# Tail and attention loop of a backward kernel: PSUM banks, eviction engine, store queues, and the order of loads and stores

## The chip, the cores and the metric

The kernel runs on one core of one Trainium2 chip. The metric is the device time of one execution in microseconds, lower is better. TensorE (PE), VectorE (DVE), ScalarE (ACT) and GpSimd (POOL) compute; SyncE (SP) only issues DMAs. SP, ScalarE and GpSimd each have a queue of DMAs of their own, and an engine's queue is worked off in order: an instruction that waits holds up everything behind it.

## The reference

The reference returns the output and nine gradients of a transformer block with modulated layer norms (batch 1, 2048 tokens, 512 features, 32 heads of 16, inner width 1792, bf16):

```
mod = silu(c) @ w_mod                      # sa, ca, ga, sb, cb, gb
h = layernorm(x) * (1 + ca) + sa
x = x + ga * attention(h, wqkv, wo)
h = layernorm(x) * (1 + cb) + sb
x = x + gb * (relu(h @ w1 + b1)**2 @ w2 + b2)
out, vjp = jax.vjp(block); return out, *vjp(grad_out)
```

The change touches the backward pass of the attention and what comes after it: with E = exp(scores), dS = (dO V^T) * E, the loop makes dV = E^T dO, dK = dS^T Q and dQ = dS K for each head. The tail makes dh1 = [dQ dK dV] Wqkv^T, the gradient of the first layer norm (output 1), dWqkv = h1^T [dQ dK dV] (output 2), and the gradients of c (output 8) and w_mod (output 9).

## The kernel before

The forward pass and the backward pass of the dense part come first and are not touched. Then two stages follow, and in both the instructions of every engine stand in the order in which the program writes them.

**The loop.** The 32 heads go in eight groups (`hg`, called heads here) of four. A head has 64 units: four blocks of 512 keys (`kc`), times 16 blocks of 128 queries in four groups (`qc`, `qi`). A unit is four score products (`psS_A`, `psS_B`, `psS_C`, line 1578), four exponentials on ScalarE (`expo`, `E_u`, line 1584), two calls of `dp_pair` (each two products `psD_u` and one product with `E_u` on VectorE, line 1600), the products into `accVK`, and a transpose of `dS_u` (`transpose_unit`), mostly by a DMA on SP's queue: 32 blocks of 128 x 128 every second unit, or 16 blocks. Two blocks of units later the transposed `dsT` is multiplied with K into `dqacc` (`dq_quad`, line 1667), which ScalarE scales and GpSimd adds up (`dq_out`, line 1685); after a head's last block the sum lies in `dQst`.

A written list of letters gives the order of these steps within a block. A counter `j` counts the calls of `dp_pair`, 128 to a head; `at(j, ...)` puts a step behind call `j`. What is put there are DMAs on ScalarE's queue (`load`, line 1560): the 22 loads of the next head (`plan_head`), the stores of `vkb` to `dVKtP`, the four stores of `dQst` to `dQc`, and towards the end pieces of what the tail reads (`pieces`) and rows of the transposed weight (`w_rows`). The DMAs of the SP and ScalarE queues share eight semaphores in turn.

**The tail.** `dh1(t)` adds 11 or 12 products of 512 columns for token tile `t` of 16 into a PSUM bank: first those whose sources are on the chip (`early7`), then `late`, of which `dq` 3 comes last. Tiles with `t % 6 < 2` have a bank of their own (`psx`); the others are halves of a two-bank tile of `psd`. For each tile ScalarE makes `xn1b` (`norm_tile`), VectorE two products with sums and a small scaling (`ln_grad`), ScalarE `tqa`, VectorE `uqa` (`dx_out`), which GpSimd's queue adds to output 1. `mod_row` spreads rows of earlier sums over the partitions (`pmod`), `wmod_grad` makes output 9 (`dwms`). `turn_vk` turns four sources on TensorE (`tokA`), `turn_dma` four more by DMA (`tokB`) and later the four of `dq` into `KS_tok`, over the weight rows that `dh1` has read. Then twelve groups of 16 products (`dwqkv`, line 1967) make dWqkv in the order `tokA`, `tokB`, `KS_tok`; between them stand the last row sums, `c_grad` with the loaded `w_mod`, and `c_out`. Each group is copied into `wqblk` (three buffers) and stored.

The names of the DMAs' sources and targets in the profile are those of the reused tiles: `ik`, `iv`, `iq`, `ido` and `qz` hold `dq` and `vk` sources in the tail.

Of the kernel before, what the change touches and what calls it, by code (L numbers as in the profile page):

```python
# [20 lines left out]
P = 128  # L21
# [13 lines left out]
def kernel(  # L35
# [1491 lines left out]
    dqw = hold.enter_context(tc.tile_pool(name="phIw", bufs=2))  # L1527
    psd = hold.enter_context(tc.tile_pool(name="psId", bufs=2, space=bass.MemoryType.PSUM))
    psx = hold.enter_context(tc.tile_pool(name="psIx", bufs=1, space=bass.MemoryType.PSUM))
# [6 lines left out]
    with ExitStack() as ph:  # L1536
        ework = ph.enter_context(tc.tile_pool(name="phIe", bufs=4))
        units = [(hg, kc, qc, qi) for hg in range(HG) for kc in range(QC) for qc in range(QC) for qi in range(4)]
        NU = len(units)
# [22 lines left out]
        def plan_head(hg):  # L1562
            j0 = (hg - 1) * 128 + 14
            loads = list(kvq_loads(hg)) + list(row_loads(hsets[hg % 2]["do"], dOT_st, hg, slice(0, n), d_st))
            for i, (to, fro) in enumerate(loads):
                at(j0 + 4 * i, load, to, fro)
            at(j0 + 40, spread_qz, hg)
# [102 lines left out]
        def dq_out(b):  # L1670
# [15 lines left out]
            if kc == QC - 1 and qc == QC - 1 and hg < HG - 1:  # L1686
                for hq in range(4):
                    r = hg % 2 * 64 + hq * DH
                    at(cur["j"] + 6 + hq, load, dQc[hg // 2, r:r + DH, :], st["dq"][32 * hq:32 * hq + DH, :])

# [23 lines left out]
        with tc.manual_schedule(engines={PE.engine, ACT.engine, DVE.engine, SP.engine, POOL.engine}):  # L1714
# [49 lines left out]
            late = (("dq", 1), ("vk", 4), ("dq", 2), ("vk", 5), ("dq", 3))  # L1764
            pds, pair = {}, {}

            def acc_of(t):
                if t not in pds:
                    if t % 6 < 2:
                        pds[t] = psx.tile([P, 512], F32, name="pdh1", tag=f"ps{t % 6}")[:]  # L1770
                    else:
                        if t % 2 == 0:
                            pair["t"] = psd.tile([P, 2, 512], F32, name="pdh2", tag="pd")
                        pds[t] = pair["t"][:, t % 2, :]
                return pds[t]
# [9 lines left out]
            def turn_vk(i):  # L1785
                pt = psd.tile([P, TT, P], BF, name="ptv", tag="pd")
                for t in range(TT):
                    PE.transpose(pt[:, t, :], xs["vk", i][:, t * P:(t + 1) * P], identb[:])
                for g in range(2):
                    DVE.tensor_copy(tokA[:, i, 8 * g:8 * g + 8, :], pt[:, 8 * g:8 * g + 8, :])  # L1790

# [39 lines left out]

    with ExitStack() as ph:
        big = ph.enter_context(tc.tile_pool(name="phJbig", bufs=1))
        rec1, rec4 = (hsets[i]["qs"].rearrange("p t e -> p (t e)").bitcast(F32) for i in range(2))
# [17 lines left out]
        def constants():  # L1852
            POOL.memset(thirty2[:], 1.0 / 32)
            POOL.tensor_copy(selb[:], identb.rearrange("p (j c) -> p j c", c=32)[:, :, 0:1].to_broadcast([P, 4, P]))
            POOL.tensor_copy(rowsb[0:97, :], sums[0:97, :])
            DVE.scalar_tensor_tensor(out=nb1[:], in0=mean1[:], scalar=-1.0, in1=rstd1[:], op0=ALU.mult, op1=ALU.mult)

# [12 lines left out]
        def wmod_grad(ic, js, k):  # L1870
            buf = dwms[:, ic % 2]
            ACT.activation(buf[:, k, :], dmodb[:, js[k], :], AF.Identity, scale=siluc_f[:, ic:ic + 1])
            if k == len(js) - 1:
                SP.dma_start(out=out_9[ic * P:(ic + 1) * P, js[0] * D:(js[-1] + 1) * D].rearrange("p (j d) -> p j d", d=D),
                             in_=buf[:, 0:len(js), :])
# [82 lines left out]
        def dwqkv(n, b, ic):  # L1958
            if n % 4 < 2:
                if n % 4 == 0:  # L1960
                    accs["p"] = psd.tile([P, 2, 512], F32, name="pwq", tag="pd")
                pw = accs["p"][:, n % 2, :]
            else:
                pw = psx.tile([P, 512], F32, name="pwx", tag=f"ps{n % 2}")[:]
            for t in range(TT):
                rhs = KS_tok[:, t, 0:D] if b == 0 else (tokA if b == 1 else tokB["t"])[:, :, t, :]
                PE.matmul(pw, h1J[:, t, ic * P:(ic + 1) * P], rhs, start=(t == 0), stop=(t == TT - 1))
            wblk = big.tile([P, D], BF, name="wqblk", tag="xn1b", bufs=3)
            rows = out_2[ic * P:(ic + 1) * P, :]
            if b == 0:  # L1970
                ACT.activation(wblk[:, 0:256], pw[:, 0:256], AF.Identity)
                DVE.tensor_copy(wblk[:, 256:512], pw[:, 256:512])
                SP.dma_start(out=rows[:, 0:D], in_=wblk[:])
            else:
                for i in range(2):
                    srcv = pw.rearrange("p (g v d) -> p g v d", v=2, d=DH)[:, :, 1 - i, :]
                    dstv = wblk[:, i * 256:(i + 1) * 256].rearrange("p (g d) -> p g d", d=DH)
                    if i == 0:
                        ACT.activation(dstv, srcv, AF.Identity)
                    else:  # L1980
                        DVE.tensor_copy(dstv, srcv)
                dst = rows[:, D:3 * D].rearrange("p (v c) -> p v c", v=2)[:, :, (b - 1) * 256:b * 256]
                SP.dma_start(out=dst, in_=wblk.rearrange("p (v c) -> p v c", v=2))

# [10 lines left out]
        with tc.manual_schedule(engines={PE.engine, ACT.engine, DVE.engine, SP.engine, POOL.engine}):  # L1995
            for g in range(3):
                load_x0(g)
            constants()
            turn_vk(1)
            last_dq(B_last, slice(3 * 512, n))  # L2000
            turn_vk(2)
            turn_vk(3)
# [5 lines left out]
            for t in range(2, 6):  # L2008
                dh1(t, early7)
                if t < 4:  # L2010
                    mod_row(3 * (t - 2))
            load_x0(3)
            for t in range(TT):
# [3 lines left out]
                ln_grad(t)  # L2017
                if t in (1, 3):
                    mod_row((t + 1) // 2)
                if t > 0:  # L2020
# [3 lines left out]
                if t >= 8:  # L2024
                    wmod_grad(t // 4 - 2, (2, 3, 4, 5), t % 4)
                if t < 8 and t % 2 == 0:
                    turn_dma("vk", 4 + t // 2)
                if t in (6, 8, 10, 11):
                    g = (6, 8, 10, 11).index(t)
                    dma(h1J[:, 4 * g:4 * g + 4, :], h1_st[:, 4 * g:4 * g + 4, :])  # L2030
                if t % 4 == 3 and t > 4:
                    row_sums(t // 4 - 1)
            for i in range(4):
                load_wmod(i)
                turn_dma("dq", i)
            order = [(b, ic) for b in (1, 2, 0) for ic in range(DC)]
            cg = [(j, ic) for j in (2, 3, 4, 5, 0, 1) for ic in range(DC)]
            for k, (b, ic) in enumerate(order):
# [16 lines left out]
                elif k < 8:  # L2055
                    wmod_grad(k - 4, (0, 1), 0)
                    wmod_grad(k - 4, (0, 1), 1)
                if k == 10:
                    c_out()

# [61 lines left out]
```

## Time and profile before

| what | value |
|---|---|
| median of 3 runs | 2514.32 us (2510.01, 2514.43 and the median) |
| profiled execution, its own time | 2511.93 us |
| its span, first to last instruction | 2510.1 us |
| TensorE busy | 2311.6 us (92%) |
| ScalarE busy | 2297.3 us (92%) |
| VectorE busy | 1812.8 us (72%) |
| GpSimd busy | 361.0 us (14%) |
| mean granted TensorE clock | 0.984 |
| loop | about 1118 to 2374 us of the span |
| tail | about 2374 to 2510 us of the span |

Busy times are of the one profiled execution; durations in what follows are from it too. A name with q behind it (ACTq, SPq) is the sequencer of that engine, which issues DMAs. A bracket behind a row gives the idle time of the engine before it and what ended it.

### The profile page before, as it was taken

The page shows a single profiled execution, that of the slowest core. Times are in us where ns is not written, and L with a number is a line of the kernel's source. Part 1 is how long each engine was busy: PE and PEld are TensorE (multiplying, and loading weights), DVE is VectorE, ACT ScalarE, POOL GpSimd, SP SyncE. Part 2 cuts the span into 40 slices and gives each one's busy share as a digit, 9 for nine tenths or more (in the row PEclk, how much of TensorE's full clock was granted, in tenths as well). Part 3 has the DMA queues.
Part 4 walks back from the last instruction along what each step waited for, and adds up shares of the span by engine and source line. Part 5 has one row for each costly group of instructions (what it writes and reads, how often), then busy time and mean ns, then how long its engine had stood idle before and what let it go on. Part 6 is the DMA issues. An engine that isn't in the chain of part 4 may idle for free.

```text
span 2510.1 us, 49480 instructions
## 1 busy us (share of the span) xinstructions
PE 2311.6 (92%) x18745; PEld 767.3 (31%) x18826; DVE 1812.8 (72%) x2366; ACT 2297.3 (92%) x3574; POOL 361.0 (14%) x393
## 2 busy tenths in 40 slices
PE   8898799989988998999999999999999999999987
PEld 3232223223322323432223322233232333223333
DVE  6555153454435454579999989999999999989864
ACT  7999999999989999539999999999999999999852
POOL 2000001211322242110111101111010110100110
PEclk9999999999999999999999999999999999999998
DMA  4467454367658765969999999999999999999975
GB/s 146 128 168 176 150 124 128 90 169 144 94 91 176 146 145 113 270 198 195 205 201 200 201 205 208 192 208 202 205 201 209 210 206 206 207 197 204 208 175 152
DMA packets 1224858, 442.37 MB, mean 176 GB/s; under 512 B 1099246, under 2 KB 1197548, under 8 KB 1224364
## 3 DMA queue, kind: packets, MB, share of 16 engines
q1 hardware_dynamic: 1189788, 398.06, 81.8%
q0 software_dynamic: 13120, 18.88, 5.4%
q10 hardware_dynamic: 21712, 22.27, 3.5%
q8 instruction: 148, 2.42, 0.4%
q14 instruction: 90, 0.74, 0.1%
HBM read 94.63 MB, written 70.78 MB: 66 GB/s over the span
## 4 chain that ended last, share of the span: by engine, by line
ACT 40%; PE 38%; issue 8%; DVE 6%; DMA 4%; SPq 1%; ACTq 1%; POOL 0%; another core or an unknown queue 0%; DVEq 0%; POOLq 0%
ACT E_u L1584 24%; ACT ET L566 12%; PE dqacc L1667 4%; PE psST L564 4%; PE psS_A L1578 3%; PE pm L232 3%; PE accVK L1640 2%; DMA dsT<-dS_u 2%; ACT dsT L1754 2%; PE psS_B L1578 2%; PE oacc L580 2%; PE psS_C L1578 2%; PE pm L413 2%; PE pm L399 2%; PE accVK L1649 2%
## 5 line engine op out<-in xcount | busy, mean ns | idle before, releaser
L1600 DVE TENSOR_TENSOR dS_u<-psD_u,E_u 128x1024 bf16<-128x1024 f32 x1024 | 1186.1, 1217 | 71.0 <-PE psD_u L1598 17.2
L566 ACT ACTIVATE ET<-psST 128x1024 bf16<-128x1024 f32 x1024 | 941.3, 1254 | 20.4 <-PE psST L564 20.2
L1584 ACT ACTIVATE E_u<-psS_A 128x512 bf16<-128x512 f32 x768 | 510.8, 665 | 11.1 <-DMA d_st<-dltT 7.3
L1584 ACT ACTIVATE E_u<-psS_B 128x512 bf16<-128x512 f32 x768 | 504.1, 656 | 13.0 <-DMA dsT<-dS_u 6.7
L1598 PE MATMUL psD_u<-iv,ido 32*128 32x512 bf16 x2048 | 408.4, 386 | 0.0
L564 PE MATMUL psST<-qt_sb,kt_sb 32*128 32x512 bf16 x2048 | 319.6, 385 | 61.2 <-ACT ET L566 46.9
L1584 ACT ACTIVATE E_u<-psS_C 128x512 bf16<-128x512 f32 x512 | 334.1, 652 | 6.6 <-DMA dsT<-dS_u 2.9
L1578 PE MATMUL psS_B<-ik,iq 32*128 32x512 bf16 x768 | 293.5, 382 | 15.9 <-ACT E_u L1584 8.6
L1578 PE MATMUL psS_A<-ik,iq 32*128 32x512 bf16 x768 | 292.1, 380 | 11.7 <-ACT E_u L1584 1.1
L1578 PEld LDWEIGHTS <-iq 32*128 32x128 bf16 x2048 | 130.3, 91 | 316.4 <-issue 298.7
L1640 PE MATMUL accVK<-dS_u,qz 128*32 128x512 bf16 x2048 | 212.5, 390 | 0.3 <-PE psD_u L1598 0.3
L580 PE MATMUL oacc<-ET,vaug 128*32 128x512 bf16 x2048 | 207.4, 395 | 3.2 <-DVE ostage L584 3.2
L1685 POOL TENSOR_TENSOR dQacc<-dQacc,dqtmp 128x512 f32<-128x512 f32 x64 | 81.3, 1270 | 852.0 <-ACT dqtmp L1680 790.3
L1649 PE MATMUL accVK<-E_u,dOs_tok 128*16 128x512 bf16 x2048 | 203.2, 386 | 0.0
L1578 PE MATMUL psS_C<-ik,iq 32*128 32x512 bf16 x512 | 194.6, 380 | 4.1 <-ACT dqtmp L1680 0.2
L564 PEld LDWEIGHTS <-kt_sb 32*128 32x128 bf16 x2048 | 86.4, 91 | 349.9 <-issue 325.4
L1667 PE MATMUL dqacc<-dsT,KS_tok 128*32 128x512 bf16 x2048 | 145.8, 382 | 17.9 <-ACT E_u L1584 3.8
L1754 ACT ACTIVATE dsT<-ptT 128x1024 bf16<-128x1024 bf16 x126 | 144.2, 1145 | 1.8 <-PE ptT L1630 1.6
L250 DVE COPY part<-pm 128x512 f32<-128x512 f32 (+2 forms) x103 | 63.5, 616 | 113.6 <-PE pm L232 103.5
L1598 PEld LDWEIGHTS <-ido 32*128 32x128 bf16 x2048 | 104.8, 91 | 99.4 <-issue 93.3
L1640 PEld LDWEIGHTS <-qz 128*32 128x32 bf16 x2048 | 57.9, 94 | 177.7 <-issue 162.8
L584 DVE COPY ostage<-oacc 128x512 f32<-128x512 f32 x32 | 22.1, 689 | 101.4 <-PE oacc L580 85.2
(417 smaller groups left out, 2512.3 us busy)
## 6 DMA issues: line engine op xcount, KB each, us to landing
p_st<-part POOLq DMA_DIRECT2D x36, 256.0 KB, 5.3
kt_sb<-qkT_st SPq DMA_DIRECT2D x124, 64.0 KB
wA<-in_B_w_dram SPq DMA_DIRECT2D x28, 256.0 KB
wB<-w1T_st SPq DMA_DIRECT2D x21, 256.0 KB
wA<-w2T_st SPq DMA_DIRECT2D x21, 256.0 KB
wB<-in_B_w_dram SPq DMA_DIRECT2D x21, 256.0 KB
p_st<-part POOLq DMA_DIRECT2D x25, 192.0 KB, 4.6
p_st<-part SPq DMA_DIRECT2D x18, 256.0 KB
```

Of the source, the lines that this page charges most:

```text
L564: PE.matmul(ps[:, hi, :], kt_sb[r:r + 32, kt * P:(kt + 1) * P], qt_sb[r:r + 32, :], start=True, stop=True, tile_position=(r, 0))
L566: ACT.activation(ET[:, 2 * pair:2 * pair + 2, :], ps[:], AF.Exp, scale=SCALE)
L580: PE.matmul(oacc[32 * hq:32 * hq + 32, :], lhsT, ET[:, hq, :], start=(kt == 0), stop=(kt == TT - 1), tile_position=(0, 32 * hq), skip_grou ...
L1578: PE.matmul(psS[:], st["q"][r:r + 32, qt * P:(qt + 1) * P], st["k"][r:r + 32, kc * 512:kc * 512 + 512], start=True, stop=True, tile_positi ...
L1584: ACT.activation(bst[u][0][:, hq, :], sst.pop((u, hq))[:], AF.Exp, scale=SCALE)
L1598: PE.matmul(psD[:, hi, :], st["do"][r:r + 32, qt * P:(qt + 1) * P], st["v"][r:r + 32, kc * 512:kc * 512 + 512], start=True, stop=True, til ...
L1600: DVE.tensor_tensor(dS_u[:, 2 * pair:2 * pair + 2, :], psD[:], E_u[:, 2 * pair:2 * pair + 2, :], ALU.mult)
L1640: PE.matmul(cur["vk"][32 * hq:32 * hq + 32, :], hst[hg]["qz"][:, qt, hq, :], bst[u][1][:, hq, :], start=(qt == 0), stop=False, tile_positi ...
L1649: PE.matmul(acc[32 * hq:32 * hq + DH, :], dOs_tok[:, qt, (hg * 4 + hq) * DH:(hg * 4 + hq + 1) * DH], E_u[:, hq, :], start=False, stop=(qt ...
L1667: PE.matmul(acc[32 * hq:32 * hq + 32, :], KS_tok[:, kc * 4 + kt, h * DH:h * DH + 32], tT[:, :, hq * 4 + kt, :], start=(kt == 0), stop=(kt ...
L1685: POOL.tensor_tensor(dst2, dst, tmp[:], ALU.add)
L1754: ACT.activation(dst, pt[:], AF.Identity)
```

## The change

In the loop, the first four loads of the next head stay at calls 14, 18, 22 and 26 of the head; the other 18 move from calls 30 to 98, four apart, to calls 50 to 111, about 3.6 apart. The four stores of dQ move from four consecutive calls (the sixth to ninth after the last sum) to calls 30, 34, 38 and 42 of the head after.

In the tail, the two-bank pool `psd` ends with the loop and four single banks (`psJn`) take its place: every token tile of `dh1`, every half of `turn_vk` and every group of `dwqkv` has a bank to itself. ScalarE alone copies dWqkv out of PSUM; `wqblk` has three buffers of its own instead of sharing them with `xn1b`. The stores of `wqblk` (but the last) and of `dwms` go to GpSimd's queue. The constants stand behind the last dQ sum on GpSimd, with the one VectorE step split off (`nb1_rows`). The `mod_row` steps move from among the early `dh1` products behind token tiles 1 to 4. The loads of `h1` come at tiles 0, 2, 3 and 4 instead of 6, 8, 10 and 11, the transposes of `tokB` at 6, 8, 10 and 12 instead of 0, 2, 4 and 6. All `w_mod` loads go ahead of the four transposes into `KS_tok`, with which they alternated. `c_grad` goes by blocks of `ic`, and `c_out` stands behind the last group instead of ahead of it. The twelve copies of `dwqkv` on VectorE are gone.

```diff
-    psd = hold.enter_context(tc.tile_pool(name="psId", bufs=2, space=bass.MemoryType.PSUM))
+        psd = ph.enter_context(tc.tile_pool(name="psId", bufs=2, space=bass.MemoryType.PSUM))
...
-                at(j0 + 4 * i, load, to, fro)
+                at(j0 + (4 * i if i < 4 else 36 + 36 * (i - 4) // 10), load, to, fro)
...
-                    at(cur["j"] + 6 + hq, load, dQc[hg // 2, r:r + DH, :], st["dq"][32 * hq:32 * hq + DH, :])
+                    at(hg * 128 + 158 + 4 * hq, load, dQc[hg // 2, r:r + DH, :], st["dq"][32 * hq:32 * hq + DH, :])
...
-                        if t % 2 == 0:
-                            pair["t"] = psd.tile([P, 2, 512], F32, name="pdh2", tag="pd")
-                        pds[t] = pair["t"][:, t % 2, :]
+                        pds[t] = banks4["p"].tile([P, 512], F32, name="pdh2", tag="pn", bufs=4)[:]
...
+        banks4["p"] = ph.enter_context(tc.tile_pool(name="psJn", bufs=4, space=bass.MemoryType.PSUM))
...
-                SP.dma_start(out=out_9[ic * P:(ic + 1) * P, js[0] * D:(js[-1] + 1) * D].rearrange("p (j d) -> p j d", d=D),
+                POOL.dma_start(out=out_9[ic * P:(ic + 1) * P, js[0] * D:(js[-1] + 1) * D].rearrange("p (j d) -> p j d", d=D),
...
-            if n % 4 < 2:
-                if n % 4 == 0:
-                    accs["p"] = psd.tile([P, 2, 512], F32, name="pwq", tag="pd")
-                pw = accs["p"][:, n % 2, :]
+            if n % 3 < 2:
+                pw = banks4["p"].tile([P, 512], F32, name="pwq", tag="pn", bufs=4)[:]
             else:
-                pw = psx.tile([P, 512], F32, name="pwx", tag=f"ps{n % 2}")[:]
+                pw = psx.tile([P, 512], F32, name="pwx", tag=f"ps{n // 3 % 2}")[:]
...
-            wblk = big.tile([P, D], BF, name="wqblk", tag="xn1b", bufs=3)
+            wblk = big.tile([P, D], BF, name="wqblk", tag="wqblk", bufs=3)
+            queue = SP if n == 11 else POOL
             if b == 0:
-                ACT.activation(wblk[:, 0:256], pw[:, 0:256], AF.Identity)
-                DVE.tensor_copy(wblk[:, 256:512], pw[:, 256:512])
-                SP.dma_start(out=rows[:, 0:D], in_=wblk[:])
+                ACT.activation(wblk[:], pw, AF.Identity)
+                queue.dma_start(out=rows[:, 0:D], in_=wblk[:])
...
-            constants()
+            nb1_rows()
             turn_vk(1)
             last_dq(B_last, slice(3 * 512, n))
+            constants()
...
-                if t < 4:
-                    mod_row(3 * (t - 2))
...
-                if t in (1, 3):
-                    mod_row((t + 1) // 2)
+                if 1 <= t < 5:
+                    mod_row(t - 1)
...
-                if t < 8 and t % 2 == 0:
-                    turn_dma("vk", 4 + t // 2)
-                if t in (6, 8, 10, 11):
-                    g = (6, 8, 10, 11).index(t)
+                if t in (6, 8, 10, 12):
+                    turn_dma("vk", 1 + t // 2)
+                if t in (0, 2, 3, 4):
+                    g = (0, 2, 3, 4).index(t)
...
             for i in range(4):
                 load_wmod(i)
+            for i in range(4):
                 turn_dma("dq", i)
...
-            cg = [(j, ic) for j in (2, 3, 4, 5, 0, 1) for ic in range(DC)]
+            cg = [(j, ic) for js in ((2, 3, 4, 5), (0, 1)) for ic in range(DC) for j in js]
...
-                if k == 10:
-                    c_out()
+            c_out()
```

More of the change, by code (lines that the diff above doesn't have):

```diff
@@ L1764 @@
             late = (("dq", 1), ("vk", 4), ("dq", 2), ("vk", 5), ("dq", 3))
-            pds, pair = {}, {}
+            pds, banks4 = {}, {}
             def acc_of(t):
@@ L1785, in turn_vk @@
             def turn_vk(i):
-                pt = psd.tile([P, TT, P], BF, name="ptv", tag="pd")
-                for t in range(TT):
-                    PE.transpose(pt[:, t, :], xs["vk", i][:, t * P:(t + 1) * P], identb[:])
                 for g in range(2):
-                    DVE.tensor_copy(tokA[:, i, 8 * g:8 * g + 8, :], pt[:, 8 * g:8 * g + 8, :])
+                    if "p" in banks4:
+                        pt = banks4["p"].tile([P, 8, P], BF, name="ptv", tag="pn", bufs=4)
+                    else:
+                        pt = psd.tile([P, 8, P], BF, name="ptw", tag="pd")
+                    for i8 in range(8):
+                        t = 8 * g + i8
+                        PE.transpose(pt[:, i8, :], xs["vk", i][:, t * P:(t + 1) * P], identb[:])
+                    DVE.tensor_copy(tokA[:, i, 8 * g:8 * g + 8, :], pt[:])
             def copy_turn(half):
@@ L1855, in constants, with nb1_rows @@
             POOL.tensor_copy(rowsb[0:97, :], sums[0:97, :])
+        def nb1_rows():
             DVE.scalar_tensor_tensor(out=nb1[:], in0=mean1[:], scalar=-1.0, in1=rstd1[:], op0=ALU.mult, op1=ALU.mult)
@@ L1976, in dwqkv @@
                     srcv = pw.rearrange("p (g v d) -> p g v d", v=2, d=DH)[:, :, 1 - i, :]
[L1977 to L1981, printed above, removed]
+                    ACT.activation(wblk[:, i * 256:(i + 1) * 256].rearrange("p (g d) -> p g d", d=DH), srcv, AF.Identity)
                 dst = rows[:, D:3 * D].rearrange("p (v c) -> p v c", v=2)[:, :, (b - 1) * 256:b * 256]
-                SP.dma_start(out=dst, in_=wblk.rearrange("p (v c) -> p v c", v=2))
+                queue.dma_start(out=dst, in_=wblk.rearrange("p (v c) -> p v c", v=2))
         def turn_dma(key, i):
```

## The prediction

> **What bounds the kernel now.** I read the page first, then busy time by stretches, then for each stretch that is not full the waits, the timeline of the engine that holds it and the chain of waits.
>
> ```profile
> ACT 40%; PE 38%; issue 8%; DVE 6%; DMA 4%; SPq 1%; ACTq 1%; POOL 0%; another core or an unknown queue 0%; DVEq 0%; POOLq 0%
> ```
>
> The chain alternates between ScalarE and TensorE, so no one engine is the bound all along. The columns of the next view are the stretch, its length, and the busy us (and instructions) of PE, weight loads, DVE, ACT and POOL, then TensorE's granted clock, DMA share, GB/s. The first two rows are two heads of the attention loop (128 steps of two products `psD_u`, called pairs here, 1.21 us each), the others the tail.
>
> ```profile
> 1273.00:1428.00 155.00, 149.34 (x1450) 47.05 (x1451) 148.55 (x129) 153.50 (x294) 17.98 (x13) 1.00 1.21 201
> 1428.00:1583.00 155.00, 146.55 (x1396) 45.47 (x1389) 143.26 (x125) 148.28 (x283) 17.98 (x13) 0.98 1.18 203
> ...
> 2374.00:2401.30 27.30, 21.54 (x193) 11.34 (x192) 12.73 (x17) 7.08 (x10) 3.79 (x5) 0.94 0.94 217
> 2401.30:2443.20 41.90, 35.88 (x171) 14.69 (x169) 33.58 (x90) 27.24 (x37) 8.49 (x7) 0.96 0.74 163
> 2443.20:2464.10 20.90, 19.97 (x96) 8.60 (x93) 9.00 (x14) 6.79 (x12) 1.20 (x1) 1.00 1.04 240
> 2464.10:2473.10 9.00, 0.04 (x2) 0.01 (x1) 2.66 (x9) 2.80 (x6) 0.00 (x0) 0.69 0.99 290
> 2473.10:2506.00 32.90, 28.62 (x111) 11.79 (x112) 15.64 (x50) 6.63 (x14) 0.00 (x0) 0.88 0.20 68
> ```
>
> In the loop ScalarE is full in one head (153.5 of 155) and 5 us short in the next. In the tail nothing is full for long, and for 9 us nothing runs but DMA. ScalarE's timeline shows where the loop's 5 us went, and the waits what stopped the tail:
>
> ```profile
> 1456.52 0.80 ACTq L1560 DMA_DIRECT2D dQc<-dQst  x1
> ...
> 1458.10 0.60 ACT L1584 ACTIVATE E_u<-psS_A 128x512 bf16<-128x512 f32 x1
> 1462.22 0.31 ACTq L1560 DMA_DIRECT2D dQc<-dQst  x1
> 1462.57 0.60 ACT L1584 ACTIVATE E_u<-psS_B 128x512 bf16<-128x512 f32 x1 [3.87 <-DMA dsT<-dS_u]
> ```
>
> ```profile
> ACT wqblk L1979 <- DMA out_dram<-wqblk: 12.8, 1, 12.8
> ...
> PE pwq L1967 <- DVE wqblk L1981: 9.9, 2, 9.0
> ...
> PE pmod L1867 <- DVE rowsb L1862: 4.4, 1, 4.4
> ...
> PE pcT L1895 <- DVE dcol L1893: 3.2, 1, 3.2
> ```
>
> The exponential did not need the transpose. The fourth dQ store stands ahead of it on ScalarE's queue, and the store waits: each DMA of the SP and ScalarE queues waits for the one eight places before it, and eight before this one is a transpose that was still moving.
>
> **The loop.** Merging the two queues' DMAs so that the eight semaphores come round in turn gives, for every DMA on ScalarE's queue, how many pairs ago the DMA eight before it was issued. Before, the fourth store of heads 0 to 5 has a 32-block transpose 10 pairs back, and head 6's third has one 9 back (and a load behind it a short one); everything else is at 12 or more. The seven places are 155 us apart, and their gaps are 0.49, 3.87, 0.46, 0.40, 2.87, 0.40 and 2.92 us, with smaller ones behind. Against 41.2 us of ScalarE in an undisturbed stretch of 41.5, the stretches around the seven places lack 0.7, 4.7, 0.5, 0.8, 3.5, 0.3 and 3.8: 14 us. Spread out, the stores have their transposes at least 15 back; the smallest distances are now 11 (two loads after the last store), 12 (five) and 14. The moved loads are as many as before, and the last lands on a plan 17 pairs (20 us) ahead of its head. A transpose took 10.3 pairs where the wait was 0.4 us and 13.2 where it was 3.87, so the seven DMAs at 11 and 12 may still wait, 0 to 4 us together. I take 2: **-12**, bounds -10 and -14.
>
> **Token tiles.** The two 512-column products that share one PSUM tile wait for each other; with single banks each waits for its own. Before, VectorE's first `dxn` starts at 2401.28 and TensorE's first `pwq` at 2443.2. Two things delay the first: TensorE waits 4.41 us for `rowsb` behind the 3.35 us reciprocal and again 0.52 us, then runs at half rate (matmuls 0.427 apart instead of 0.216). With the four `pmod` products moved behind tokens 1 to 4, the early products end at about 2392.6, and then the late ones wait for `dq` 3, whose first rows land at 2396.1 by the trace's landing events. POOL's dQ sums come up to 2.2 us earlier, as the constants now stand behind them, but the stores to `dq` 3 wait for loads of 512 KB landing every 2.4 us, so I gain nothing there. The first `dxn` is at 2396.9: **-4.4**.
>
> From there TensorE has 145 products of 0.216 (31.3), three row sums of 0.55 (1.65), four `pmod` (0.9) and, after a wait of 3.5 us, a half-rate window of 3.4 us (1.7; bounds 0 and 1.7): 35.5, so `pwq` starts at 2431.8, 11.4 before; **-7.0** beyond the first term. VectorE needs 2.27 a token (2410.70 to 2412.97, where it waited for nothing), 36.3 for sixteen; it ends at 2433.2 and TensorE, six banks ahead, waits for it only at `row_sums(3)`, one group later. ScalarE's two to three passes (0.72, 0.72, 0.61) fit into 2.27. The early `h1` loads and the later transposes of `tokB` are all issued by about 2425; `tokB` is first read at 2446.
>
> **dWqkv.** Before, 2443.2 to 2506.0 is 62.8: twelve groups of 3.46 (41.5), row sum 0.55, two `ptot` 1.72, pair waits 0.93 twice, 8.96 for the store, 2.4 of half rate behind that, `pcT` 3.5, half rate again 1.9. The first three terms, 43.8, remain: **-19.0**. The store's wait goes because the SP queue held it behind the `w_mod` loads and four transposes (2446.5 to 2467.7); on POOL it stands behind uqa and `dwms` stores alone, 1.2 us each by the uqa rows, two per group of 3.46. ScalarE takes the whole eviction: 2 x 0.38 or 0.60 plus 1.32 for `dwms`, 2.1 of 3.46. Six banks cover a late eviction by some 20 us.
>
> What is late next is `KS_tok`, read from group 8 on, 29 us after 2431.8: w_mod's 3.1 MB, the transposes' 2.1 and about 2.4 MB of stores go first. At 290 GB/s (the 9 us row) that is 26 us, at 240 (the row before it) 32: 0 to 3 us late, I take 1. The end: last matmul to the span's end was 4.1; now a 0.60 eviction replaces 0.39 + 0.44, and the `dcol` row is sent 0.4 later and POOL's store of group 10 lands near the end: 0 to +1, I take 0.7.
>
> The Trainium skill (DMA: Bandwidth & Descriptors, Issuing engines are not separate DMA queues) says that transfers from SP, ScalarE and GpSimd share the same 16 engines, so a second queue adds no bandwidth. The trace agrees: share 0.99 and 290 GB/s in the 9 us while one queue moved. The move buys order only, and that is all the sum uses.
>
> **Sum.** -12 - 4.4 - 7.0 - 19.0 + 1 + 0.7 = -40.7 on the profiled execution's 2511.9 (span 2510.1 and 1.8 around it): 2471.2. On the median of 2514.3, which is 2.4 above it, 2473.6. I say 2473.
>
> **The rivals.** *Stores land late.* Three `wqblk` buffers let a store take 10.4 us. Queued behind 512 KB of `dwms` while loads run, it may take 16 (the worst store before went 8 us from the end of the transposes): each group is then 16/3 = 5.3, 22 us lost, 2495. For it: 27 POOL transfers where there were 8. Against: 1.19 to 1.30 us for a uqa store with VectorE 80% busy, 4.9 to landing. Chance 0.10.
>
> *POOL's issue becomes the bound.* VectorE's work may hold POOL up while it writes a store's descriptors. The longest such row of the trace is 2.05 us (a `p_st` row at 1011): two per group are 4.1 against 3.46, twelve times 0.64 is 8 us lost, 2481. Against: the uqa rows stay within 1.30. Chance 0.04. The Trainium skill (SBUF — State Buffer, SBUF: two separate sides) states this rule: VectorE's two-port modes lock GpSimd out of a port that its descriptors need, 0.62 us alone becoming 3.1 beside a copy. By it two stores take 6.2 per group, 33 us lost, 2506 as an estimate from that page; the uqa rows do not bear it out.
>
> *The stores still wait in the loop.* If a transpose keeps taking 13 pairs, the DMAs at 11 and 12 wait 1 to 2 pairs each and what follows is late too: the loop gives 4 instead of 12, 2481. Chance 0.10.
>
> *Slower.* The loads now stand 3.6 pairs apart instead of 4, and some 45 of ScalarE's DMAs have a transpose 11 to 16 back. Should the transposes, SP's queue being 18.3 of every 19.3 us under way, complete only after 15 pairs (18 us), the waits come to about 33 pairs, 40 us, which eats both gains: 40 - 14 - 28.7 is -3. At 15.5 they are about 50 pairs, 60 us, and the kernel is at 2531. Against: before has ten such places at 14 pairs and 28 at 15, and the trace shows no gap over 0.2 us at them. Chance 0.04.
>
> *The token tiles go on as before*, each held by the trip from TensorE over VectorE to ScalarE and back, and the banks change nothing: -7.0 is lost, 2480. For it: `tqa` waited for `c12a` 15 times, 18.7 us. Against: at 2410 to 2417 the same trip took 2.27 a token. Chance 0.10.
>
> **How the numbers follow.** Forecast 0.66, bounds of its unknowns 2468 to 2478 (loop -14 to -10, half rate 0 to 1.7, `KS_tok` 0 to 3, end 0 to 1). The base moves it: from the fastest run, 2510.0, the low end is 2464, and 3 more go off for short waits that the sum leaves in. Upwards it takes in the cases at 2480 and 2481 and reaches into the late stores: 2461 to 2492. That leaves out about 0.12: most of the late stores and the slower case. A run can tell 0.2% from no change. Every case but the slower one is faster by more than 0.2%, 0.96; I take 0.03 from it for what no row shows: faster 0.93, same 0.02, slower 0.05.
>
> **What would show it.** Right: no exponential waiting over 1 us for `dsT`, where there were three; the first `pwq` some 35 us after the first `dxn`, not 42; no gap over 1 us between the twelve `pwq` and `pwx` groups and 44 to 45 us for them; `KS_tok` landed 30 us after the first `pwq`. Wrong: POOL rows over 2 us, ScalarE waiting for `out_dram<-wqblk`, or ScalarE's DMA rows ahead of new gaps at pairs 623, 751 and 931 to 947, the places at 11 and 12.

## The result, and the profile after

The kernel after takes 2493.1 us (median of 4 runs, 2489.3 to 2495.0) where the kernel before, beside it, takes 2512.2 (4 runs, 2506.2 to 2514.4): a ratio of 0.9926, with a 95% interval of 0.9903 to 0.9949. It is 19 us faster, where 41 were forecast. The profiled execution took 2491.6 us with a span of 2489.4, 20.7 less than the span before. By the marks that the prediction used, these 20.7 us come from here:

| stretch (us) | before | after | moved | forecast |
|---|---|---|---|---|
| loop, first to last exponential | 1254.7 | 1253.6 | -1.1 | -12 |
| last exponential to first `dxn` | 27.35 | 23.28 | -4.1 | -4.4 |
| first `dxn` to first `pwq` | 41.95 | 39.05 | -2.9 | -7.0 |
| twelve groups | 62.75 | 50.56 | -12.2 | -19 + 1 |
| last product to end | 4.15 | 4.10 | 0 | +0.7 |

(The other 0.35 us lie ahead of the loop.) Busy time by stretches, columns as in the prediction:

```profile
1428.00:1583.00 155.00, 149.81 (x1428) 46.71 (x1425) 146.41 (x128) 151.93 (x290) 17.96 (x13) 0.98 1.21 204
1273.00:1428.00 155.00, 149.09 (x1446) 46.81 (x1443) 148.57 (x129) 153.28 (x293) 17.96 (x13) 1.00 1.20 201
2372.40:2395.70 23.30, 19.65 (x190) 10.96 (x189) 12.99 (x16) 5.82 (x9) 3.80 (x5) 1.00 0.97 222
2395.70:2434.80 39.10, 36.10 (x174) 14.96 (x173) 33.79 (x90) 28.15 (x40) 8.27 (x8) 0.96 0.98 203
2434.80:2464.90 30.10, 30.10 (x144) 13.16 (x140) 22.92 (x61) 14.31 (x31) 9.91 (x14) 1.00 1.12 257
2464.90:2468.80 3.90, 0.03 (x1) 0.01 (x1) 0.00 (x0) 2.22 (x5) 1.27 (x2) 0.79 1.04 292
2468.80:2489.40 20.60, 16.34 (x63) 6.90 (x65) 0.00 (x0) 3.36 (x7) 2.21 (x4) 0.83 0.12 41
```

The loop's second head is 3 us short of ScalarE's full 155 where it was 7 short, so the first row is better. The first eight groups run without a pause (30.10 of 30.10). Then TensorE stands for 3.9 us while DMA is full, and runs on at a clock of 0.83. TensorE's waits in the tail, and the queue that the first of them looks at:

```profile
PE pwx L1970 <- DMA KS_tok<-iq: 3.9, 1, 3.9
PE pmod L1872 <- ACT dmodb L1873: 3.0, 3, 1.3
```

```profile
2437.40 12.45 SPq L1991 DMA_TRANSPOSE KS_tok<-qz  x1
2449.89 5.26 SPq L1991 DMA_TRANSPOSE KS_tok<-ik  x1
2455.19 4.80 SPq L1991 DMA_TRANSPOSE KS_tok<-ido  x1
2460.04 4.79 SPq L1991 DMA_TRANSPOSE KS_tok<-iq  x1
```

The last transpose lands at 2468.7, 34 us after the first `pwq` (forecast 30). The 9.0 us that TensorE waited before for an eviction held up by a store (`pwq` for `wqblk`) are gone from its list, and so is the wait for `rowsb`. In the loop, ScalarE's timeline where a store of dQ stands now, and where a new gap stands:

```profile
1248.04 0.31 ACTq L1560 DMA_DIRECT2D ido<-dOT_st  x1
1248.26 0.79 ACT L1584 ACTIVATE E_u<-psS_A 128x512 bf16<-128x512 f32 x1
1248.44 1.08 ACTq L1560 DMA_DIRECT2D dVKtP<-vkb  x1
1249.62 0.60 ACT L1584 ACTIVATE E_u<-psS_C 128x512 bf16<-128x512 f32 x1 [0.58 <-PE accVK L1649]
...
1470.18 0.60 ACT L1584 ACTIVATE E_u<-psS_C 128x512 bf16<-128x512 f32 x1
1470.27 0.33 ACTq L1560 DMA_DIRECT2D dQc<-dQst  x1
1470.66 0.62 ACT L1584 ACTIVATE E_u<-psS_A 128x512 bf16<-128x512 f32 x1
```

The store of dQ at 1470 costs nothing: the exponentials go on 0.48 us apart, where a 3.87 us gap stood at 1462. But a store of `vkb` right behind a load takes 1.08 us on the queue instead of 0.31, and the next exponential is 0.58 late.

### The profile page after: what moved, and what is told of

The parts are those of the page before. It is cut to its first block, busy times and chain, and to the rows that moved or that the text cites. A ratio compares the mean times of both kernels' runs of the same rounds, so it can differ in the third digit from the quotient of the medians.

```text
span 2489.4 us, 49493 instructions
## 1 busy us (share of the span) xinstructions
PE 2313.2 (93%) x18745; PEld 767.8 (31%) x18826; DVE 1809.5 (73%) x2354; ACT 2301.3 (92%) x3582; POOL 372.5 (15%) x412
## 4 chain that ended last, share of the span: by engine, by line
ACT 42%; PE 38%; issue 8%; DVE 6%; DMA 3%; SPq 1%; ACTq 1%; POOL 0%; another core or an unknown queue 0%; DVEq 0%; POOLq 0%
ACT E_u L1584 24%; ACT ET L566 13%; PE dqacc L1667 4%; PE psST L564 4%; PE psS_A L1578 3%; PE pm L232 3%; ACT dsT L1754 2%; PE accVK L1640 2%; PE psS_B L1578 2%; PE oacc L580 2%; PE pm L413 2%; PE pm L399 2%; PE psS_C L1578 2%; PE accVK L1649 2%; PE pm L488 1%
## 5 line engine op out<-in xcount | busy, mean ns | idle before, releaser
L1578 PE MATMUL psS_A<-ik,iq 32*128 32x512 bf16 x768 | 293.5, 382 | 12.8 <-ACT E_u L1584 2.7
```

What stands on the lines that cost most here:

```text
L1578: PE.matmul(psS[:], st["q"][r:r + 32, qt * P:(qt + 1) * P], st["k"][r:r + 32, kc * 512:kc * 512 + 512], start=True, stop=True, tile_positi ...
```

## What the loop lost: half-rate windows

The loop's ScalarE waits of before are mostly gone and the loop is hardly shorter. What came in their place shows in three stretches of 3.41 us, the length of the steps in which the profile's granted clock changes:

```profile
1449.99:1453.40 3.41, 3.29 (x27) 0.98 (x24) 3.16 (x4) 3.41 (x8) 0.19 (x1) 1.00 0.98 167
1453.40:1456.81 3.41, 3.41 (x21) 1.09 (x20) 2.86 (x3) 2.93 (x5) 0.00 (x0) 0.50 1.32 201
1456.81:1460.22 3.41, 3.21 (x37) 1.25 (x39) 2.44 (x3) 2.87 (x5) 0.00 (x0) 1.00 1.10 251
```

TensorE is 96% busy, ScalarE full; then the granted clock is 0.50 for exactly one step (a half-rate window, or window for short), and ScalarE loses 0.48 us in it and 0.54 in the next: 1.0 us for each such window. Nothing waited before it. TensorE's timeline shows what stood at its edge:

```profile
1452.80 0.37 PE L1578 MATMUL psS_B<-ik,iq 32*128 32x512 bf16 x1
1453.29 0.95 PE L1630 MATMUL ptT<-identb,dS_u 128*128 128x128 bf16 x8
1454.17 0.60 PE L1649 MATMUL accVK<-E_u,dOs_tok 128*16 128x512 bf16 x4
```

`ptT` are the transposes of `dS_u` that TensorE makes itself, two groups of eight in every 16 pairs. These, the first group, start 0.11 us ahead of the step's edge, after a pause of 0.12; from there the products take 0.60 us instead of 0.39. The before profile has two windows of this kind in the loop (at 1573 and 1594), the after profile six. Two theories follow. **Chance:** windows fall on a grid of 3.413 us that has nothing to do with the kernel, and it depends on the execution how many edges meet the start of a `ptT`. **Caused:** the new order makes them. The experiments below separate these, and settle the tail's two shortfalls. Behind each median stands its ratio to the kernel before, run on the same chip, with the 95% interval; the kernel before had medians of 2515.0 to 2519.8 there.

## The experiments

**The two halves alone.** `loop_only` is the kernel before with the first two edits of the diff, `tail_only` the kernel after without them.

> The kernel before with the loop's two edits alone (loads of the next head and stores of dQ moved). Theory A, the forecast's: the seven places where ScalarE's queue waits are worth 12 us, so this kernel takes 10 to 14 us off the kernel before, and the gain went missing in the profile of after only by chance. Theory B: with the waits gone TensorE falls into half-rate windows it did not have before, and residual waits of two DMAs standing together take the rest, so the loop gives 0 to 4 us, with the last exponential 1 to 3 us earlier than in before. If the half-rate windows belong to the order of the work, this profile has them at the same places as the kernel after (1453, 1474, 1873, 1959, 1979, 2174, 2262, 2334 us); if they fall by chance, at others.

> The kernel after with the loop's loads and stores of dQ put back where they stood before, so that only the tail is changed. From the two profiles the tail is worth 19.2 us (136.2 us from the last exponential to the end before, 117.0 after). Theory A: 17 to 20 us off the kernel before, some 12 us slower than the kernel after would be in a typical run. Theory B: the same 17 to 20 us off the kernel before and within 4 us of the kernel after. Its loop is that of before, so gaps of ScalarE of 3.87, 2.87 and 2.92 us at 1462, 1934 and 2244 us should be there again; half-rate windows at the places of before if they belong to the order, at others if by chance.

Measured: `loop_only` 2513.3 (12 runs), 0.9979 of before (0.9960 to 0.9998), so 5 us; `tail_only` 2498.5, 0.9908 (0.9884 to 0.9932), 23 us. The tail is worth more than the 17 to 20 us that both theories gave it, and the loop's 5 us lie between the theories, at less than half of the forecast's 12; the interval reaches from 0.5 to 10 us. The windows of `loop_only` stand at 1221, 1358, 1566, 1672, 2034, 2256, 2317 and 2337. Only the last is where the after profile has one (2334, the loop here being 3 us later by then), though every instruction of the loop is the same; and `tail_only`, with the loop of before, has eight starts where before has five.

**Repeats.** `after_rep` and `before_rep` are the two kernels unchanged.

> The kernel after once more, with another profile. Half-rate windows of TensorE in the loop come in two kinds in the six profiles so far: some behind a stretch in which TensorE was idle, and others in a full rhythm, each beginning within 0.2 us of the start of the first ptT products of a block, on a grid of 3.413 us that runs through the whole execution. Theory A (chance): where the grid falls against the loop's rhythm of 19.4 us differs from execution to execution, so this profile has 2 to 6 such windows in the loop at other places than 1453, 1474, 1959, 1979, 2174 and 2334 us, the loop takes 1249 to 1257 us, and its ScalarE is idle for 13 to 16 us outside the windows. Theory B (the change makes the windows): 5 or more at the same places. Time 2483 to 2496, 0.985 to 0.993 of the kernel before.

> The kernel before once more, for another profile. Theory A (windows by chance): 2 to 8 windows at the start of the first ptT in the loop at other places than 1573 and 1594 us, the loop 1254 to 1266 us long, ScalarE idle 22 to 24 us outside the windows, and three gaps of 2.5 us or more behind stores of dQ. Rival (the order of before makes fewer windows than that of after): at most two again, the loop at 1254 to 1256.

Measured: `after_rep` 2493.1 (6 runs), 0.9895 of before (0.9870 to 0.9921), with eight windows at `ptT` (1547, 1629, 1649, 1670, 1963, 1984, 2318 and 2339) and a loop of 1260.0, both above what was expected (and 16.7 us of idle time outside the windows, for 13 to 16), but at places of their own; `before_rep` 2512.7 in one run, with six, at other places than 1573 and 1594, and a loop of 1260.6. The rival that the order of before makes fewer windows falls. Of the three gaps that were expected behind stores of dQ it has two (4.16 and 2.84 us), and 21.0 us of idle time outside the windows, for 22 to 24. With the profiles of all kernels whose loop is that of before (4) or of after (7), adding up ScalarE's pauses in the trace by place gives (mean, lowest to highest):

| per loop (us) | before's loop | after's loop |
|---|---|---|
| windows at the start of `ptT` | 5.5 (2 to 9) | 6.1 (2 to 8) |
| length of the loop | 1261.6 (1254.7 to 1265.8) | 1256.2 (1249.6 to 1260.0) |
| ScalarE idle, 16 pairs behind each of the seven dQ places | 13.8 (11.0 to 18.0) | 4.0 (3.0 to 5.4) |
| idle at pairs 621, 749 (16 each) and 931 to 957 | 0.7 (0.7 to 0.8) | 3.7 (1.6 to 6.7) |
| idle elsewhere, without the loop's first 30 pairs | 15.6 (10.5 to 19.4) | 16.6 (10.2 to 21.0) |

The stores gave 9.8 us back; 3.0 came again at the places that the prediction named, where by its merging a DMA stands 11 or 12 pairs behind its transpose; the last row is nearly the same in both, but varies by 10 us from execution to execution. The profile of before that the forecast was made on had the lowest value of that row for its loop (10.5), the after profile 14.9. (Idle time outside the windows, here and below, leaves out each window and half a step behind it.)

**A product in the pause.** `warm_turn` moves one of the two extra products of `keep_warm` from ahead of the second `ptT` of a block to ahead of the first; `before_warm` does the same to the kernel before.

```diff
-            "s0 s1 q s2 e0 e1 D s3 D e2 s4 e3 t1 e4 q T1 D "
-            "s5 s6 e5 f f t2 e6 s7 T2 e7 D s8 e8 D f f s9 e9 q q s10 "
+            "s0 s1 q s2 e0 e1 D s3 D e2 s4 e3 f t1 e4 q T1 D "
+            "s5 s6 e5 f t2 e6 s7 T2 e7 D s8 e8 D f f s9 e9 q q s10 "
```

> The kernel after with one of the two extra products that stand ahead of the second ptT of a block moved ahead of the first ptT. Theory A (the clock is decided by whether TensorE is idle at the instant where the grid falls; the instant ahead of the first ptT is a 0.1 us pause while its bank comes free): with a product in the pause the windows at the first ptT go, at most 2 windows in the loop's full rhythm, ScalarE idle 16 to 21 us in the loop instead of 25 to 30, the loop at 1242 to 1249 us; 4 to 9 us off the kernel after. Rival 1 (it is the transposing products themselves that count as idle): windows as before, within 2 us. Rival 2: with one product less ahead of the second ptT the windows move there, in the same number; no gain.

> The kernel before with one of the two extra products ahead of the second ptT moved ahead of the first, and nothing else; its loop against that of the run warm_turn shows the loop's two edits without the windows that fall by chance. Theory A (the edits are worth the waits of the stores, about 8 us of ScalarE's idle time outside windows, where the forecast had 12): no window at the start of the first ptT, ScalarE idle outside the windows 23 to 26 us against 16.7 in warm_turn, the loop 1257 to 1263 us against 1251.6. Rival (the forecast's size): 28 to 30 us of idle time, the loop 1263 or more. Time 2 to 7 us below the kernel before.

Measured: `warm_turn` 2486.0, 0.9875 of before (0.9849 to 0.9901); `before_warm` 2508.3, 0.9970 (0.9954 to 0.9987). No window at `ptT` is left in either profile, though edges still fall there. At one of them (2119.41, the `ptT` starting at 2119.36) in `warm_turn`:

```profile
2116.00:2119.41 3.41, 3.41 (x27) 0.89 (x24) 3.17 (x4) 3.41 (x8) 0.00 (x0) 1.00 1.16 257
2119.41:2122.82 3.41, 3.36 (x34) 1.52 (x33) 3.31 (x4) 3.41 (x7) 0.00 (x0) 1.00 1.17 215
```

The clock stays at 1.00 and ScalarE full. Over all profiles, an edge from 0.06 us ahead of to 0.19 us behind the start of the first `ptT` was followed by a half-rate window 71 times of 85 in twelve loops with the pause, and 0 times of 13 in four loops with the product in it. So these windows need the pause and an edge that falls at its end or just behind, and how many edges do so is chance: 2 to 8 in seven profiles of one loop. In time, `before_warm` is clear of the kernel before; `warm_turn` is 5 us below `after_rep` by the ratios, with intervals that overlap. The sizes were missed, though: the loop of `warm_turn` is 1251.6 us (1242 to 1249 expected), with 27.2 us of idle time, of which 10.5 in windows that follow a step with TensorE at most 85% busy; and `before_warm` has 1250.3, below what both theories gave, and less than `warm_turn`, which it was expected to exceed by 5 to 11 us. Outside the windows its idle time is 20.9 us (23 to 26 expected) against 16.7. With one profile each, these two do not show the worth of the loop's edits; the table above and `loop_only` do.

**ScalarE's DMAs apart.** `apart` moves stores of `vkb` and weight rows off the pairs of other loads.

```diff
-                    at(cur["j"] + 4, load, dVKtP[hg][:, part], hst[hg]["vk"][:, part])
+                    at(cur["j"] + (4, 5, 2, 4)[kc], load, dVKtP[hg][:, part], hst[hg]["vk"][:, part])
...
-            at((4 + i // 8) * 128 + 106 + 4 * (i % 8), load, w_rows(j)[r], ...)
+            at((4 + i // 8) * 128 + 109 + 4 * (i % 8), load, w_rows(j)[r], ...)
```

> The kernel after with three kinds of DMA of ScalarE's queue in the loop moved by one to three pairs, so that no store of vkb and no row of the weight stands on the same or the next pair as a load. Theory A (the second of two DMAs issued together takes 1.05 us of ScalarE's queue instead of 0.31 and costs an exponential about 0.55 us each time): the gaps of 0.45 to 1.0 us outside the half-rate windows go, ScalarE idle outside the windows 10 to 12 us instead of 14 to 16; 2 to 5 us off the kernel after. Rival (the wait belongs to the transposes under way, wherever the DMA stands): as many such gaps at other places, no gain beyond 1 us.

Measured: 2487.0, 0.9874 (0.9842 to 0.9905); in the same session `after_rep` had 0.9895. Idle time outside the windows is 12.8 us (after's loop: 14.1 to 16.7), so some 2 us went, and the short gaps behind stores of `vkb` with it; the gap of about 1 us at pairs 931 to 957 stayed. The direction is theory A's, short of its 10 to 12 us; in time it cannot be told from nothing.

**The token tiles.** `pmod_two` gives the four `pmod` products two banks in turn.

```diff
-            pm = psx.tile([P, 512], F32, name="pmod", tag="px")
+            pm = psx.tile([P, 512], F32, name="pmod", tag=("px", "accVK")[k % 2])
```

> The kernel after with the four spreading products pmod alternating between two PSUM banks instead of one. Theory A (the single bank ties TensorE to the pace of tokens 1 to 4, because each dmodb copy stands on ScalarE behind the tqa of its token): the three waits of 1.34, 0.80 and 0.86 us of pmod for dmodb go, TensorE runs ahead, and the first pwq comes 36 us after the first dxn instead of 39: 2 to 3.5 us off the kernel after. Rival (VectorE's 2.27 us a token sets the pace, or the next wait takes its place): the first pwq stays 38 to 39 us after the first dxn, no gain.

Measured: 2485.7 (6 runs), 0.9860 (0.9834 to 0.9886). The stretch from first `dxn` to first `pwq` in `pmod_two`:

```profile
2390.43:2426.73 36.30, 34.24 (x174) 14.54 (x172) 33.17 (x90) 27.99 (x40) 8.24 (x8) 1.00 1.01 218
```

36.3 us, as expected, and 36.3 again in `tail_mix` below (36.9 and 37.9 in the last two kernels); all eight profiles of the changed tail with one bank have 39.0 to 39.8. But theory A is only half of it. Two short waits of the three are left (2.1 us, where one bank leaves 3.0 to 3.8), and the granted clock is 1.00: `pmod_two` and `tail_mix` have no half-rate window in this stretch, and each of the eight has one, worth some 1.7 us. `best_sp`, with two banks and one window, takes 37.9. So the second bank is worth 1 to 2 us by the waits; that the window went because of it is not shown, since with two banks `best_sp` still has one and `all_four` two. In time the ratio is below that of `after_rep`, with overlapping intervals.

**KS_tok.** `ks_first` puts the four transposes into `KS_tok` ahead of the `w_mod` loads, `tail_mix` mixes them (two transposes, two pairs of loads, two transposes, two pairs) and has the two `pmod` banks.

```diff
 # ks_first
+            for i in range(4):
+                turn_dma("dq", i)
             for i in range(4):
                 load_wmod(i)
-            for i in range(4):
-                turn_dma("dq", i)
```

> The kernel after with the four transposes into KS_tok ahead of the w_mod loads instead of behind them. Theory A (the transposes wait in SP's queue behind 3.1 MB of loads): KS_tok landed 22 to 28 us after the first pwq instead of 34, the gap of 3.9 us before group 8 and the half-rate window behind it go, 5 to 6.5 us off the kernel after; c_grad waits for w_mod and may lose 0 to 2 of it at the end. Rival (the transposes themselves and the stores beside them are what is slow, about 5 us each whatever stands ahead): landed 32 to 34 us after, gain below 1.5 us; or c_grad becomes what ends last, and the kernel is no faster.

> The kernel after with the pmod products in two banks and with two transposes into KS_tok, two of the four w_mod pairs of loads, the other two transposes, and the other two pairs, in this order. Theory A (both earlier gains hold, and the loads come early enough for c_grad): first pwq 36 to 37 us after the first dxn, KS_tok landed 27 to 30 us after the first pwq and no gap before group 8, twelve groups in 44 to 45 us, last product to end 4.1 to 5: tail 106 to 108 us instead of 117. Rival (c_grad still waits for the last w_mod loads): the end takes 6 to 8 us, tail 109 to 111.

Measured: `ks_first` 2489.4, 0.9878 (0.9850 to 0.9906); `tail_mix` 2479.8, 0.9850 (0.9824 to 0.9875). In `ks_first` the groups take 43.98 us without a pause, but then `c_grad` ends last, the second of its rivals; VectorE's and TensorE's waits:

```profile
DVE junk L1892 <- DMA ik<-in_w_mod_dram: 17.4, 1, 17.4
```

```profile
PE pcT L1900 <- DVE dcol L1898: 3.7, 1, 3.7
```

The end takes 7.1 us instead of 4.1. Mixed, the groups take 43.98 too and the end 4.1: a tail of 104.3 us (106 to 108 expected) where the forecast had 107.5. It is theory A without its rival.

**Whose queue the stores are in.** `stores_sp` (with the loop of before) and `after_sp` (with that of after) put the stores of `wqblk` and `dwms` back on SP's queue, behind the loads and transposes.

```diff
-            queue = SP if n == 11 else POOL
+            queue = SP
...
-                POOL.dma_start(out=out_9[ic * P:(ic + 1) * P, ...
+                SP.dma_start(out=out_9[ic * P:(ic + 1) * P, ...
```

> The kernel after with the loop's loads and stores of before and with the stores of wqblk and dwms back on SP's queue, where they stand behind the w_mod loads and the four transposes, so only the banks, the eviction on ScalarE and the order of loads differ from before in the tail. Theory A, the forecast's (the 9 us gap goes because the stores leave SP's queue): ScalarE waits for a store of wqblk until 31 to 33 us after the first pwq, TensorE for ScalarE, and the twelve groups take 5 us or more longer than with the stores on GpSimd's queue (44.9 to 50.8). Rival (six single banks alone cover it: group 9 is the first that needs a bank whose eviction waits for a store, and TensorE reaches it 31 to 34 us after the first pwq anyway): ScalarE waits as long, but the groups take no more than 2 us longer.

> The kernel after with nothing changed but the stores of wqblk and dwms, back on SP's queue. Theory A (on GpSimd's queue the stores run beside the transposes into KS_tok and slow them; behind them on SP's queue they do not, and six banks cover ScalarE's wait): the last three of these transposes take 2 to 3 us each instead of 3.9 to 6.8, TensorE has no gap before group 8, the twelve groups take 44 to 45 us, the tail 105 to 110 us. Rival (the run stores_sp was a lucky one: with the loop of after the transposes take 4 to 5 us again): groups 45 to 51 us, tail 108 to 118 as in the runs with the stores on GpSimd's queue.

Measured: `stores_sp` 2491.3, 0.9903 (0.9878 to 0.9929); `after_sp` 2490.4, 0.9896 (0.9871 to 0.9921). ScalarE waits as it did before, in `after_sp`:

```profile
2466.33 0.66 ACT L1980 ACTIVATE wqblk<-pwq 128x256 bf16<-128x256 f32 x2 [13.78 <-DMA out_dram<-wqblk]
```

and TensorE does not notice: the twelve groups take 43.98 us in both runs, the shortest there is. SP's queue in `after_sp` shows why:

```profile
2447.79 8.67 SPq L1991 DMA_TRANSPOSE KS_tok<-qz  x1
2456.51 2.22 SPq L1991 DMA_TRANSPOSE KS_tok<-ik  x1
2458.78 2.45 SPq L1991 DMA_TRANSPOSE KS_tok<-ido  x1
2461.28 2.58 SPq L1991 DMA_TRANSPOSE KS_tok<-iq  x1
```

With no stores beside them the last three transposes take 2.2 to 2.6 us instead of 4.8 to 5.3. In the five profiles with the tail as changed and the stores on GpSimd's queue they take 3.9 to 6.8, and the groups 44.9, 44.9, 50.6, 50.8 and 51.7. The rival of `stores_sp` and theory A of `after_sp` hold: single banks removed the 9 us, and the move of the stores cost 1 to 8 us by the profiles. (The kernel before has six banks for the groups too, but four of them in two tiles of two: its wait of 8.96 us is that of the sixth group for the eviction of the fifth, which has the other half of its tile.) In time this is not seen: `after_sp` has the ratio of `after_rep`, whose groups took 44.9 us, and executions of one kernel lie 10 us apart.

**Together.** `all_four` has the two `pmod` banks, the mixed order, the product ahead of the first `ptT` and the DMAs apart; `best_sp` the same with the stores on SP's queue in place of the mixed order.

> The kernel after with all that helped on its own: pmod in two banks, transposes into KS_tok mixed with the w_mod loads, one extra product ahead of the first ptT, and the DMAs of ScalarE's queue apart. If the gains add up: loop 1244 to 1250 us, tail 104 to 107, 2465 to 2476 in time, 0.981 to 0.984 of the kernel before. If the gaps of the loop come back at other places, as in the run warm_turn (16.7 us of idle time outside the windows), loop 1250 to 1254 and 0.983 to 0.986.

> The kernel after with the pmod products in two banks, the stores of wqblk and dwms back on SP's queue with the order of its loads as in after, one extra product moved ahead of the first ptT, and the DMAs of ScalarE's queue in the loop apart. If the parts add up: loop 1244 to 1250 us, first pwq 36 to 37 us after the first dxn, groups 44 us, tail 103 to 108, 2466 to 2478 in time, 0.980 to 0.985 of the kernel before. If the loop falls back as in warm_turn, 0.985 to 0.988.

Measured: `all_four` 2481.6, 0.9870 (0.9841 to 0.9899), in its profile a loop of 1244.4 and a tail of 108.2; `best_sp` 2480.4, 0.9853 (0.9828 to 0.9879), loop 1252.7, tail 105.7. The loop of `all_four` is as expected in its profile, but not the tail and the time; `best_sp` has the loop and the ratio of its second case. Neither beats `tail_mix`. By their ratios the three are 0.25 to 0.45% below `after_rep`, and their intervals overlap with its own; against the kernel before all are clear.

## Why the prediction was wrong, point by point

**The loop, -12.** The size of the idle time at the seven places was well read (13.5 us in that profile, 13.8 on the mean), but in the profile that was read the mechanism holds at three of them only. The gaps of 3.87, 2.87 and 2.92 us stand behind a store that waits. The other four, 0.40 to 0.49 us, stand behind the first store of their head, which follows a load by 0.4 us, and the fourth store, said to be the one that waits, passes at once. One of them, in the before profile:

```profile
1615.04 0.33 ACTq L1560 DMA_DIRECT2D iqs<-q_st  x1
1615.46 1.19 ACTq L1560 DMA_DIRECT2D dQc<-dQst  x1
1616.69 0.60 ACT L1584 ACTIVATE E_u<-psS_B 128x512 bf16<-128x512 f32 x1 [0.46 <-issue]
...
1620.14 0.31 ACTq L1560 DMA_DIRECT2D dQc<-dQst  x1
```

These are two DMAs issued together, as in `apart`, so the "10.3 pairs" that a transpose was said to take came from gaps that stand at another store. The three long gaps hold 12 of the 14 us, so this alone moved the sum little. The step that failed in size is what it left: "0 to 4 us together. I take 2". At the places of dQ 4.0 stayed, half of it at head 6, and 3.7 are at pairs 621, 749 and 931 to 957: 7.7 together, of which about 2 are what undisturbed stretches have too (0.2 to 0.3 in 16 pairs). At head 6 a moved store stands right behind a load of the tail's pieces; its row takes 1.05 us in the after profile, and an exponential comes 0.45 late. For this the sum had no term, only for the distance to a transpose. The prediction had listed the other pairs under "wrong", with 4 instead of 12 for the loop as a rival at 0.10; by the means the loop gives 5.4. The other 4 us by which the profile fell short of this are chance: the forecast put one execution's half-rate windows down as a property of the kernel.

**First `dxn`, -4.4.** Right (-4.1), for the reason given.

**Token tiles, -7.0.** TensorE's products and the half-rate window were about right: in the after profile it is busy for 36.0 of the 39.0 us, where the terms add up to 35.5. (The `pwq` at 2431.8 stands only 34.9 behind the `dxn` at 2396.9: 0.6 us of the shortfall are a slip in that sum.) The step that failed is "four `pmod` (0.9)": only their own time was counted, not that all four share a bank which ScalarE empties once a token, behind `tqa`. That is the trip over VectorE and ScalarE of the rival "token tiles go on as before", on four tiles instead of sixteen, and the waits took 3.0 us. The moved step should have had its bank's reader named.

**dWqkv, -19.0.** The 43.8 us of bare work was right: 43.98 in six profiles. The reason was half wrong. "The store's wait goes because the SP queue held it" and now stands on GpSimd's: `after_sp` shows that the wait for the store may stay, all 13.8 us of it, as long as enough single banks lie between it and TensorE. The prediction used this cover for ScalarE's evictions and not for the store itself.

**`KS_tok`, +1.** The estimate of 26 to 32 us from bytes and GB/s was the right size, and in two of five profiles it held. In the other three, 6 to 7 us were lost, for a gap of 4 to 5 us and the half-rate step behind it. The sum took the stores' bytes in, but not that stores issued beside the transposes would hold up SP's queue at each of them. The Trainium skill (DMA: Bandwidth & Descriptors, Issuing engines are not separate DMA queues) was cited for the move buying order only; the trace agrees, and goes on: the order that it bought was the worse one, 4.8 to 5.3 us a transpose against 2.2 to 2.6.

**The end, +0.7.** It was 0.

**The rivals and the range.** Late stores on GpSimd's queue and GpSimd's issue did not occur: ScalarE waits for no `wqblk` store (for `dwms` stores it waits 6.5 us in all), and GpSimd's rows of these stores stay below 0.75 us. The slower case did not occur. The range missed because the shortfalls were priced as alternatives, 2480 or 2481 each, when three of them came together: 7 us in the loop, 4 in the token tiles and, in three profiles of five, 6 at `KS_tok`, which above 2473 is 2490.

## What to carry to other kernels

Before a move of stores to another queue is credited, ask what those stores will run beside: here a wait of 14 us behind enough PSUM banks was free, and stores let out early slowed the loads that TensorE read next. For a step that is moved, name not only its own time but the reader that frees its bank. And take the base of a forecast from several profiles where it can be had: the rows of one execution hold its luck, here up to 10 us.

## What the runs showed of the hardware that was not expected

TensorE's clock goes to half in steps of 3.413 us on a grid that runs through the whole execution, and a pause of about 0.1 us is enough if an edge falls from 0.06 us ahead of its end to 0.19 behind it: the step ahead is 96% busy. The Trainium skill (TensorE: Matmul & The Clock Gate, What's actually happening) gives such a free-running window of 3413 ns, which the trace agrees with, and a half clock after an idle window, which it does not: most of the 71 windows here followed a step with TensorE 96 to 98% busy, and with a single product in the pause none came at 13 such edges.

Windows of this kind come in rows of two or three, 20.5 us apart (1453.4 and 1473.9; 1958.6 and 1979.1). The rhythm of a pair of blocks is 16 times 1.21, 19.4 us; a window adds 1.0 to 1.1, and 20.48 is just six steps of the grid, so the next `ptT` tends to meet an edge again. This last step is worked out, not tried.
